# Three of four tile groups transposed by VectorE and transfers instead of TensorE, ahead of the third layer

## The chip, the cores and the metric

The kernel runs on one core of a Trainium2 chip. The metric is device time in microseconds. The kernel before took 707.68, 710.18 and 1081.44 us in three runs (median 710.18); the profiled execution took 706.28 us, of which the profile's span, from the first to the last instruction, is 704.5 us.

## The reference

The input u has 2048 positions of 512 channels. Two blocks follow each other, each ahead of a layer norm and added to its input:

```python
h  = u + ssm(layernorm(u))          # a long convolution by FFT, plus a skip term
h2 = h + mlp(layernorm(h))

def mlp(x):                         # w1, w2: 512x512, w3: 512x1792, w4: 1792x512
    g  = gelu(layernorm(x) @ w1)    # layer 1
    hs = shift(g) @ w2              # four quarters of the channels, shifted by +1 -1 +2 -2 positions; layer 2
    x1 = x + hs
    return x1 + gelu(layernorm(x1) @ w3) @ w4   # layers 3 and 4
```

Only the second block is touched here, and of it the way from x1 to layer 3, and the output.

## The kernel before, in words

The positions are held in 16 tiles of 128 positions by 512 channels (`h[:, j, :]`), in four groups q of four tiles. In a tile the 128 positions are not neighbours: position 16 p + j lies in row p of tile j up to a fixed order of the four row quarters (`ov`, line 1422), so that a shift by a position is a change of tile.

Numbers go into TensorE as a high and a low part (`split`, `gelu`, `halve`: ScalarE makes the high part, VectorE subtracts it for the low one), and a product is three matmuls (`PROD`, line 1170). Each part is a tile of 128 x 512 from the pool `slab`; temporaries come from the pool `tm` under the tags x (14 tiles) and g (6). TensorE writes into eight banks of PSUM: four that rotate (`bank`) and four that hold accumulators (`wide_bank`).

The first part of the program is the convolution, ordered by a planner (`Plan`). From about 310 us on comes `mixer_phase` (line 1127), whose order on TensorE, VectorE, ScalarE and GpSimd is that in which the Python code issues the instructions (`InOrder`): each engine works through its queue in that order. Transfers are issued by SyncE, some of the last output by ScalarE.

- Layer 1 (`layer1`, line 1219) and layer 2 (`layer2`, line 1257) are interleaved by hand in lines 1402 to 1420. `layer2(j)` writes x1 of tile j (`xq[j]`); `stats2` and `norm2` turn it into its layer norm, in place.
- Layer 3 needs the channels as rows, so each group is transposed by `turn2(q)` (line 1306): for each of four channel blocks c, four 128 x 128 transposes on TensorE against the identity into one bank, and one ScalarE copy into the tile `FT[q, c]` (128 channels by 512 positions).
- Layer 3 works on pairs of groups, as a 2 x 2 block product with seven products instead of eight (Strassen and Winograd): the operands are sums and differences of the blocks (`sums2`, line 1327) which `halve` splits, seven for each of two channel halves, so 28 slabs to a pair.
- The steps s = 0 to 13 (line 1520) run over seven pairs of column blocks of w3, for the first pair of groups (s = 0 to 6) and then for the second (7 to 13). A step does `layer3a(s)` (products a, b, c, e), layer 4 of the step before for its first half (`layer4a`), `layer3b(s)` (products f, d, g), and the second half (`layer4b`). Each product goes into a rotating bank, from which VectorE adds it (`plus`). Weights are loaded by `raw3` and `raw4` on SyncE, and split by `load3` and `load4`.

Group 0 is turned between layer1(2, 0) and layer1(2, 1) (line 1407), and its blocks b11 and b21 are halved after layer2(6) (lines 1408 to 1410). Group 1 is turned after layer2(10) (line 1411). Groups 2 and 3 belong to the second pair and are turned during the steps of the first: group 2 in step 2 (line 1541), group 3 half in step 3 and half in step 4 (line 1548); their sums are formed in steps 4 and 5, and halved around step 6 (`fresh`). In `todo` and `some` (line 1341) VectorE and ScalarE instructions are parcelled out between other work.

`store(j)` (line 1479) writes a finished tile to DRAM in four transfers of 32 rows each: on SyncE for the first pair, on SyncE and ScalarE in turn for the second.

Of the kernel before, what the change touches and what calls it, by code (L numbers as in the profile page):

```python
# [11 lines left out]
F32 = mybir.dt.float32  # L12
# [3 lines left out]
ALU = mybir.AluOpType  # L16
# [1110 lines left out]
def mixer_phase(ctx, tc, cst, h, out, finish, w3, w4):  # L1127

    nc = InOrder(tc)
    pool = lambda name, bufs, **kw: ctx.enter_context(tc.tile_pool(name=name, bufs=bufs, **kw))  # L1130
    sl = pool("slab", 45)
    tm = pool("tm", 6)
    w1p = pool("wrap", 1)
    sm = pool("sm", 2)
    ps = pool("ps2", 4, space=PSUM)
    pa = pool("pacc", 1, space=PSUM)
    ident = cst["ident"]
    NFT = F // 128

    def slab(name):  # L1140
        return sl.tile([128, 512], F32R, tag="slab", name=name)
# [1 line left out]
    def slot(i):  # L1143
        return cst["slab"](i)

    def tmp(name, tag):
        return tm.tile([128, 512], F32, tag=tag, name=name, bufs={"x": 14, "g": 6}[tag])

    def bank(name):
        return ps.tile([128, 512], F32, tag="bank", name=name)  # L1150

    def wide_bank(i, name):
        return pa.tile([128, 512], F32, tag=f"acc{i}", name=name)
# [7 lines left out]

    def gelu(b, name):

        hi, lo, g = slab(f"{name}h"), slab(f"{name}l"), tmp(f"g{name}", "g")
        nc.scalar.activation(hi, b, AF.Gelu_apprx_tanh)
        nc.scalar.activation(g, b, AF.Gelu_apprx_tanh)
        nc.vector.tensor_tensor(lo, g, hi.bitcast(F32), ALU.subtract)
        return hi, lo
# [6 lines left out]
    _, _, rr, nb = cst["norm"]  # L1175
# [30 lines left out]
    def norm1(q):  # L1206
        XL[q] = []
        for j in range(q * 4, q * 4 + 4):
            t = tmp(f"xl{j}", "x")
            if (q == 0 and j % 2) or (q == 3 and j != 14):  # L1210
                nc.vector.tensor_scalar(t, h[:, j, :], mv[:, j, 0:1], r12[:, j : j + 1], ALU.subtract, ALU.mult)
            else:
                nc.scalar.activation(t, h[:, j, :], AF.Identity, scale=r12[:, j : j + 1], bias=off12[:, j : j + 1])
            XL[q].append(t)
# [34 lines left out]
    def h1_block(f, j, k):  # L1249
        if 0 <= j < 16:  # L1250
            return H1[j // 4, f][k][:, j % 4 * 128 : j % 4 * 128 + 128]
        return wrap[k][WRAP[f, j] // 4][:, WRAP[f, j] % 4, :]

    xq = {}
    mv2 = {}

    def layer2(j):
        q, i = divmod(j, 4)
        b = bank(f"l2_{j}")
        n = 0  # L1260
        for f, sh in enumerate((-1, 1, -2, 2)):
            for wi, xi in PROD:
                nc.tensor.matmul(b, h1_block(f, j + sh, xi), W2[f][wi], start=(n == 0), stop=(n == 11))
                n += 1
        x1 = tmp(f"x1_{j}", "x")
        nc.vector.scalar_tensor_tensor(x1, h[:, j, :], r1[:, j : j + 1], b, ALU.mult, ALU.add)
        xq[j] = x1
        if j < 8:
            residual(j), stats2(j)

    def residual(j):
        (nc.gpsimd if j < 12 else nc.vector).tensor_tensor(h[:, j, :], h[:, j, :], xq[j], ALU.add)

    def stats2(j):
        q, i = divmod(j, 4)
        if q not in mv2:
            mv2[q] = sm.tile([128, 4, 2], F32, tag="mv2", name=f"mv2_{q}")
        st = sm.tile([128, 6], F32, tag="bst", name=f"st1_{j}")
        nc.vector.bn_stats(st, xq[j])
        nc.vector.bn_aggr(mv2[q][:, i, :], st)  # L1280
# [16 lines left out]
    def norm2(q):  # L1297
        for op in norm2_ops(q):
            op()
# [3 lines left out]
    half = NFT // 2  # L1303
    FT, XC, W3, W4 = {}, {}, {}, {}

    def turn2(q, cs=range(4), wide=True):

        tiles = [xq[q * 4 + i] for i in range(4)]
        for c in cs:
            b = wide_bank(c, f"x1t{q}_{c}") if wide else bank(f"x1t{q}_{c}")  # L1310
            for i, t in enumerate(tiles):
                nc.tensor.transpose(b[:, i * 128 : i * 128 + 128], t[:, c * 128 : c * 128 + 128], ident)
            FT[q, c] = tmp(f"ft{q}_{c}", "x")
            nc.scalar.copy(FT[q, c], b)

    def sub(out, a, b):
        nc.vector.tensor_tensor(out, a, b, ALU.subtract)
        return out

    def halve(src, pair, name, c, low=nc.vector):  # L1320

        hi, lo = slab(f"{name}{pair}{c}h"), slab(f"{name}{pair}{c}l")
        nc.scalar.copy(hi, src)
        low.tensor_tensor(lo, src, hi.bitcast(F32), ALU.subtract)
        XC[pair, name, c] = hi, lo

    def sums2(pair, c):

        S = FT[pair, "sums", c] = {}
        ft = lambda i, k: FT[pair * 2 + i, 2 * k + c]  # L1330
        t = lambda n: tmp(f"{n}_{pair}{c}", "xg"[pair == 0])

        def first():
            S.update(b11=ft(0, 0), b21=ft(0, 1), b22=ft(1, 1), t1=sub(t("t1"), ft(1, 0), ft(0, 0)))

        return [first, lambda: S.update(t3=sub(ft(1, 0), ft(1, 1), ft(1, 0))),
                lambda: S.update(t2=sub(t("t2"), S["b22"], S["t1"])), lambda: S.update(t4=sub(t("t4") if pair else S["b21"], S["b21"], S["t2"]))]
# [70 lines left out]
    for n in ("b11", "b21"):  # L1408
        for c in range(2):
            halve(FT[0, c + 2 * (n == "b21")], 0, n, c)  # L1410
    layer2(7), norm2(1), layer2(8), layer2(9), layer2(10), turn2(1)
    rest = []
    for c in range(2):
        t1, t3, t2, t4 = sums2(0, c)
# [7 lines left out]
    ov = out.rearrange("(a c j) d -> c a j d", c=4, j=16)  # L1422
    acc, H3, U = {}, {}, {}

    def prod(s, name, w, xk):
        b = bank(f"l3{name}_{s}")
        for n, (c, wi, xi) in enumerate((c, wi, xi) for c in range(2) for wi, xi in PROD):
            nc.tensor.matmul(b, W3[s][w][wi][:, c * 128 : c * 128 + 128], XC[s // half, xk, c][xi], start=(n == 0), stop=(n == 5))
        return b
# [10 lines left out]
        return lambda: nc.vector.tensor_tensor(lo, src, hi.bitcast(F32), ALU.subtract)  # L1440

    def layer3a(s):
        U[s] = [tmp(f"u{i}_{s}", "g") for i in range(4)]
        one, two, three, last = U[s]
        nc.scalar.copy(one, prod(s, "a", "a11", "b11"))
        if s == 0:

            f, e, c = (prod(s, n, *o) for n, o in (("f", ("a12", "b21")), ("e", ("s1", "t1")), ("c", ("s3", "t3"))))
            plus(last, f, one)
            for i in (0, 2, 1, 3):  # L1450
                rest[i]()
            load3(1, nc.vector, range(1))
            plus(two, prod(s, "b", "s2", "t2"), one)
            plus(three, c, two)
            plus(one, e, three)
            plus(two, e, two)
            U[s] = last, two, three, one
            return
        plus(two, prod(s, "b", "s2", "t2"), one)
        plus(three, prod(s, "c", "s3", "t3"), two)  # L1460
        b = prod(s, "e", "s1", "t1")
        plus(last, b, three)
        plus(two, b, two)
# [13 lines left out]
        return gelu3(s, 0, 1, two)  # L1477

    def store(j):
        for c in range(4):  # L1480
            queue = nc.scalar if j >= 8 and c % 2 else nc.sync
            queue.dma_start(ov[c][:, j, :], h[c * 32 : c * 32 + 32, j, :])

    def layer4(s, q, i, b, first, last):
        for k in range(2):
# [34 lines left out]
    for s in range(2 * half):  # L1520
        turn, last = s + 1 == half, s + 1 == 2 * half
        layer3a(s)
        if turn:
            fresh(("b11", "t2", "t3", "t1"))
        if last:
            load4(s)
        else:
            load3(s + 1, *((nc.gpsimd,) if s else (nc.vector, range(1, 3))))
        if s + 2 < 2 * half:
            raw3(s + 2)  # L1530
        if s:
            layer4a(s - 1)
        if s == 0:
            for j in range(8, 12):
                residual(j)
        if s == 1:
            for j in range(8, 12):
                stats2(j)
            todo.extend(norm2_ops(2)), some(11)
        if s == 2:  # L1540
            turn2(2, range(4), False)
            for j in range(12, 16):
                if j > 13:
                    residual(j)
                stats2(j)
            todo.extend(norm2_ops(3)), some(11)
        if s == 3 or s == 4:
            turn2(3, (s - 3, s - 1), False)
        if s == 4 or s == 5:
            todo.extend(sums2(1, s - 4))  # L1550
            some(4)
        late = layer3b(s)
        if not last and s:
            load4(s), raw4(s + 1)
        if s + 2 < 2 * half:
            sum3()
        if s:
            layer4b(s - 1, late)
        else:
            late()  # L1560
        some(4)
        if s == 1:
            residual(12), residual(13)
        if turn:
            fresh(("b21", "t4", "b22"))
# [45 lines left out]
```

## Time and profile before

| | before |
|---|---|
| runs | 707.68, 710.18, 1081.44 us |
| profiled execution | 706.28 us |
| its span | 704.5 us |
| TensorE busy | 667.0 us (95%) |
| VectorE busy | 539.7 us (77%) |
| ScalarE busy | 413.1 us (59%) |
| GpSimd busy | 393.9 us (56%) |
| granted TensorE clock, mean | 0.992 |

How to read the profile's lines: PE is TensorE's matmuls, PEld its weight loads, DVE VectorE, ACT ScalarE, POOL GpSimd, SP SyncE; SPq is SyncE's queue, which issues transfers. All times are microseconds from the start of the span, or nanoseconds where it says ns. An instruction is named by the tile that it writes and those that it reads, as in `x1t<-ident,x`. Where the kernel's helper records an instruction, all of them bear one line number (L87), so groups are told apart by their tiles: `x1t` are the banks of `turn2`, `ft` its result, `l3a` to `l3g` the seven products of layer 3, `l` the rotating banks of layers 1, 2 and 4, `acc` the accumulators of layer 4, `u` the temporaries of layer 3. In square brackets stands how long the engine was idle before an instruction, and what ended it. The chain that ended last is followed back from the last instruction, at each step to what released it. A matmul's shown duration overlaps with the next one's.

### The profile page before, as it was taken

What the parts mean: (1) busy time and instruction counts of PE and PEld (TensorE: products, weight loads), DVE (VectorE), ACT (ScalarE), POOL (GpSimd) and SP (SyncE); (2) the same over time, 40 slices, a digit from 0 to 9 for tenths busy, and PEclk for the clock granted to TensorE, in tenths of its full rate; (3) what the DMA queues carried; (4) which work ended last, traced back from release to release, by engine and by line L of the source; (5) the groups of instructions that cost most, each with busy time, mean ns of one, the idle gap of its engine ahead of it and who ended that gap; (6) DMA issues with size and microseconds to landing.
All of it is one profiled execution on the core that took longest, in us unless ns stands there. A gap on an engine that the chain in (4) does not pass through costs nothing.

```text
span 704.5 us, 16738 instructions
## 1 busy us (share of the span) xinstructions
PE 667.0 (95%) x6894; PEld 522.0 (74%) x6894; DVE 539.7 (77%) x934; ACT 413.1 (59%) x701; POOL 393.9 (56%) x407
## 2 busy tenths in 40 slices
PE   5878999999999989989999999999999999999997
PEld 5865666663776774848888888888888888888886
DVE  6998899999999898878764889846568954554544
ACT  7888778765889875245646346554545544444330
POOL 1889587967999897302555404555433655543310
PEclk9999999999999999999999999999999999999999
DMA  8830653010301133010010001221111352111004
GB/s 215 268 121 3 197 166 78 3 47 32 63 2 47 33 92 107 1 61 1 1 30 31 1 16 45 61 60 54 39 59 31 87 154 60 51 52 48 10 21 120
DMA packets 44912, 45.19 MB, mean 64 GB/s; under 512 B 4900, under 2 KB 31524, under 8 KB 44836
## 3 DMA queue, kind: packets, MB, share of 16 engines
q1 hardware_dynamic: 44068, 43.07, 21.0%
q10 hardware_dynamic: 768, 1.05, 0.6%
q8 instruction: 54, 0.88, 0.5%
q14 instruction: 22, 0.18, 0.1%
HBM read 35.72 MB, written 8.39 MB: 63 GB/s over the span
## 4 chain that ended last, share of the span: by engine, by line
PE 63%; DVE 17%; ACT 9%; DMA 4%; issue 3%; POOL 2%; SPq 1%; DVEq 0%; ACTq 0%; POOLq 0%
PE l L87 23%; PE acc L87 11%; PE bank L87 9%; ACT pt L87 5%; DVE at L87 3%; DVE u L87 3%; DVE cs L87 3%; PE l3c L87 3%; PE l3f L87 3%; PE l3e L87 3%; PE l3d L87 3%; PE l3b L87 3%; PE l3g L87 3%; PE l3a L87 3%; DVE sn L87 2%
## 5 line engine op out<-in xcount | busy, mean ns | idle before, releaser
L87 ACT ACTIVATE pt<-pt 128x1056 f32<-128x1056 int32 x64 | 69.9, 1092 | 17.2 <-POOL pt L87 7.8
L87 POOL TENSOR_TENSOR pt<-p,s 128x512 int32<-128x512 int32 x64 | 71.5, 1133 | 5.6 <-DVE sn L87 5.3
L87 PE MATMUL bank<-at,tbs 128*64 128x128 f32 (+1 forms) x768 | 64.5, 317 | 2.0 <-DVE at L87 1.0
L87 PEld LDWEIGHTS bank<-at,tbs 128*64 128x64 f32 x768 | 46.3, 138 | 18.8 <-ACT at L87 2.3
L87 PEld LDWEIGHTS bank<-ident 128*128 128x128 f32 x438 | 54.4, 204 | 7.2 <-issue 4.4
L87 PE MATMUL bank<-ident 128*128 128x128 f32 x438 | 58.4, 292 | 0.0
L87 PE MATMUL bank<-u,ms 64*128 64x128 f32 x736 | 49.4, 281 | 4.8 <-POOL u L87 2.0
L87 PEld LDWEIGHTS bank<-u,ms 64*128 64x128 f32 x736 | 43.7, 187 | 9.8 <-POOL u L87 3.1
L87 POOL TENSOR_TENSOR cs0w<-raw,cs0w 128x512 fp32r<-128x512 f32 x7 | 9.1, 1299 | 64.4 <-ACT cs0w L87 64.4
L87 DVE TENSOR_TENSOR h<-h,l 128x512 f32<-128x512 f32 x48 | 32.6, 687 | 14.7 <-PE l L87 14.7
L87 DVE TENSOR_TENSOR u<-u,l3f 128x512 f32<-128x512 f32 x14 | 9.6, 686 | 44.5 <-PE l3f L87 44.5
L87 POOL TENSOR_TENSOR cs1w<-raw,cs1w 128x512 fp32r<-128x512 f32 x7 | 9.1, 1299 | 61.0 <-ACT cs1w L87 61.0
L87 DVE TENSOR_TENSOR cs<-pt,amx 128x512 f32<-128x512 f32 x64 | 41.2, 680 | 2.4 <-ACT pt L87 1.8
L87 PE MATMUL bank<-cs 128*32 128x64 f32 x1024 | 32.7, 224 | 8.1 <-DVE cs L87 6.3
L87 PEld LDWEIGHTS bank<-cs 128*32 128x32 f32 x1024 | 24.2, 111 | 20.7 <-ACT kt L87 4.3
L87 ACT COPY at<-bank 128x512 f32<-128x512 f32 x40 | 24.7, 624 | 24.8 <-PE bank L87 24.8
L87 ACT ACTIVATE pt<-pt,halfpi 128x1056 f32<-128x1056 f32 x32 | 37.8, 1182 | 0.7
L87 DVE STREAM_TRANSPOSE at<-bank 128x512 f32<-128x512 f32 (+1 forms) x40 | 35.0, 909 | 3.5 <-PE bank L87 3.5
L87 ACT ACTIVATE u<-u 128x512 f32<-128x512 f32 x56 | 35.4, 633 | 1.8
L87 DVE TENSOR_TENSOR amx<-E,amx 128x896 f32<-128x896 f32 (+1 forms) x32 | 30.7, 959 | 5.6 <-ACT amx L87 5.4
L87 POOL TENSOR_TENSOR sn<-pt,amp 128x512 f32<-128x512 f32 x27 | 32.7, 1210 | 2.8 <-ACT pt L87 1.4
L87 PE MATMUL bank<-sn 128*32 128x64 f32 x1024 | 31.9, 223 | 2.2 <-DVE sn L87 1.6
(1161 smaller groups left out, 2096.1 us busy)
## 6 DMA issues: line engine op xcount, KB each, us to landing
raw<-in_B_w_dram SPq DMA_DIRECT2D x28, 256.0 KB, 2.6
h<-in_A_u_dram SPq DMA_DIRECT2D x32, 128.0 KB, 4.2
h<-in_A_u_dram SPq DMA_DIRECT2D x16, 256.0 KB, 4.2
rawa<-in_B_w_dram SPq DMA_DIRECT2D x14, 256.0 KB, 2.7
rawb<-in_B_w_dram SPq DMA_DIRECT2D x14, 256.0 KB, 2.7
ms<-in_mm_dram SPq DMA_DIRECT2D x4, 768.0 KB, 10.7
out_dram<-h SPq DMA_DIRECT2D x48, 64.0 KB, 1.7
xs<-far SPq DMA_DIRECT2D x10, 256.0 KB, 2.9
```

The lines of the kernel that those rows point to most:

```text
L87: ins = f(*args, **kw)
```

## The change

For groups 0, 2 and 3 `turn2` no longer uses TensorE, PSUM and ScalarE. VectorE transposes each tile in blocks of 32 x 32 within its four row quarters (four instructions of 128 x 512), and the blocks change rows by way of a DRAM buffer `via[q]`: four transfers write it (each run 512 bytes), four read it back (each run 2 KB) over the tiles of x1. All eight are issued by SyncE. The numbers come back in an order in which a channel block c lies in runs of 32 numbers, `turned` names it, and `natural` restores the order of positions where the sums and halves are formed. `FT[q, c]` is now such a view and no tile of its own.

Group 1 keeps TensorE (`turn2_wide`), and ScalarE copies its result over the tiles of x1, in the same order. Group 3 is turned wholly in step 3.

The tiles under the tag x become four fixed tiles of 128 x 2048, `XQ`, used in turn by the norms of layer 1, by x1, by the block transposes and by the sums of the second pair. The pool g goes from 6 to 5 tiles, and slab from 45 to 44. `store` writes a tile in two transfers of 64 rows.

```diff
-    sl = pool("slab", 45)
+    sl = pool("slab", 44)
...
+    dp = pool("via", 1, space=bass.MemoryType.DRAM)
+    via = {q: dp.tile([128, 2048], F32, name=f"via{q}") for q in (0, 2, 3)}
...
-    def tmp(name, tag):
-        return tm.tile([128, 512], F32, tag=tag, name=name, bufs={"x": 14, "g": 6}[tag])
+    def tmp(name):
+        return tm.tile([128, 512], F32, tag="g", name=name, bufs=5)
+
+    XQ = [w1p.tile([128, 4 * 512], F32, name=f"xq{i}") for i in range(4)]
+    X1 = {0: XQ[3], 1: XQ[1], 2: XQ[2], 3: XQ[0]}
+    quarter = lambda t, i: t[:, i * 512 : i * 512 + 512]
+    turned = lambda t, q: t.rearrange("p (a c i t) -> p c a i t" if q == 1 else "p (a i c t) -> p c a i t", a=4, c=4, i=4)
+    natural = lambda t: t.rearrange("p (i a t) -> p a i t", i=4, a=4)
...
-            t = tmp(f"xl{j}", "x")
+            t = quarter(XQ[{3: 0, 0: 1, 1: 2, 2: 0}[q]], j % 4)
...
-        x1 = tmp(f"x1_{j}", "x")
+        x1 = quarter(X1[q], i)
...
-    def turn2(q, cs=range(4), wide=True):
+    def turn2(q):
+
+        x, t = X1[q], XQ[{0: 2, 2: 3, 3: 1}[q]]
+        for i in range(4):
+            nc.vector.transpose(quarter(t, i).rearrange("p (b c t) -> p c b t", b=4, c=4),
+                                quarter(x, i).rearrange("p (c b t) -> p c b t", c=4, b=4))
+            nc.sync.dma_start(via[q].rearrange("p (b i x) -> p b i x", b=4, i=4)[:, :, i, :],
+                              quarter(t, i).rearrange("p (b x) -> p b x", b=4))
+        for a in range(4):
+            nc.sync.dma_start(quarter(x, a), via[q].rearrange("(a d) (b x) -> a b d x", a=4, b=4)[a])
+        for c in range(4):
+            FT[q, c] = turned(x, q)[:, c]
+
+    def turn2_wide(q):
 
         tiles = [xq[q * 4 + i] for i in range(4)]
-        for c in cs:
-            b = wide_bank(c, f"x1t{q}_{c}") if wide else bank(f"x1t{q}_{c}")
+        for c in range(4):
+            b = wide_bank(c, f"x1t{q}_{c}")
             for i, t in enumerate(tiles):
                 nc.tensor.transpose(b[:, i * 128 : i * 128 + 128], t[:, c * 128 : c * 128 + 128], ident)
-            FT[q, c] = tmp(f"ft{q}_{c}", "x")
-            nc.scalar.copy(FT[q, c], b)
+            FT[q, c] = turned(X1[q], q)[:, c]
+            nc.scalar.copy(FT[q, c], natural(b))
...
-        nc.scalar.copy(hi, src)
-        low.tensor_tensor(lo, src, hi.bitcast(F32), ALU.subtract)
+        nc.scalar.copy(natural(hi), src)
+        low.tensor_tensor(natural(lo), src, natural(hi).bitcast(F32), ALU.subtract)
...
-        t = lambda n: tmp(f"{n}_{pair}{c}", "xg"[pair == 0])
+        home = lambda n: quarter(XQ[(3, 1)[c]], "t1 t2 t4".split().index(n)) if pair else tmp(f"{n}_{pair}{c}")
+        t = lambda n: home(n).rearrange("p (a i t) -> p a i t", a=4, i=4)
...
-    layer2(7), norm2(1), layer2(8), layer2(9), layer2(10), turn2(1)
+    layer2(7), norm2(1), layer2(8), layer2(9), layer2(10), turn2_wide(1)
...
     def store(j):
-        for c in range(4):
-            queue = nc.scalar if j >= 8 and c % 2 else nc.sync
-            queue.dma_start(ov[c][:, j, :], h[c * 32 : c * 32 + 32, j, :])
+        for c in (0, 2):
+            queue = nc.scalar if j >= 8 and c else nc.sync
+            queue.dma_start(ov[c : c + 2, :, j, :], h[c * 32 : c * 32 + 64, j, :])
...
         if s == 2:
-            turn2(2, range(4), False)
+            turn2(2)
...
-        if s == 3 or s == 4:
-            turn2(3, (s - 3, s - 1), False)
+        if s == 3:
+            turn2(3)
```

More of the change, by code (lines that the diff above doesn't have):

```diff
@@ L1162, in gelu @@
     def gelu(b, name):
-        hi, lo, g = slab(f"{name}h"), slab(f"{name}l"), tmp(f"g{name}", "g")
+        hi, lo, g = slab(f"{name}h"), slab(f"{name}l"), tmp(f"g{name}")
         nc.scalar.activation(hi, b, AF.Gelu_apprx_tanh)
@@ L1442, in layer3a @@
     def layer3a(s):
-        U[s] = [tmp(f"u{i}_{s}", "g") for i in range(4)]
+        U[s] = [tmp(f"u{i}_{s}") for i in range(4)]
         one, two, three, last = U[s]
```

## The prediction

> **What bounds the kernel now.** The page comes first: span, busy shares and the chain of work that ended last.
>
> ```profile
> span 704.5 us, 16738 instructions
> PE 667.0 (95%) x6894; PEld 522.0 (74%) x6894; DVE 539.7 (77%) x934; ACT 413.1 (59%) x701; POOL 393.9 (56%) x407
> PE 63%; DVE 17%; ACT 9%; DMA 4%; issue 3%; POOL 2%; SPq 1%; DVEq 0%; ACTq 0%; POOLq 0%
> ```
>
> The busy share is an average, so the second view is the same chain in order of time, around the four second transposes (x1t). Columns: start, duration, what.
>
> ```profile
> 371.46 1.75 PE x1t L87 x16
> 373.21 21.86 PE l L87 x96
> 395.07 1.78 PE x1t L87 x16
> ...
> 422.79 1.67 PE l3c L87 x6
> ...
> 451.70 1.75 PE x1t L87 x16
> 453.45 1.37 PE l3f L87 x6
> ...
> 473.87 0.87 PE x1t L87 x8
> ...
> 495.19 0.87 PE x1t L87 x8
> ```
>
> Each piece starts where the one before ends: TensorE sets the end here. Group 0 is the piece at 371.46, group 1 (which stays) 395.07, group 2 451.70, group 3 the two halves. The waits of TensorE's weight loads from 360 to 530 us say how near another engine is:
>
> ```profile
> PEld l3c L87 <- DVE u L87: 0.5, 1, 0.5
> PEld l L87 <- DVE h_3l L87: 0.2, 1, 0.2
> ```
>
> Two waits only, both for VectorE. So no slack shows, and VectorE is the next bound, at 422 us above all.
>
> **What leaves TensorE.** 48 transposes: 1.75 us in group 0, 1.75 in group 2, 0.87 twice in group 3, together 5.24 us. The tile view gives their single durations:
>
> ```profile
> L87 PE MATMUL x1t<-ident,x x64: 270/272/308, 371.3 to 495.8; 128*128 128x128 f32 x64
> L87 ACT COPY ft<-x1t x16: 586/592/640, 372.5 to 496.1; 128x512 f32<-128x512 f32 x16
> ```
>
> They overlap: sixteen take 1.75 us on the chain, 109 ns each, and only that can be saved. ScalarE loses 12 copies of 0.59 us, which are on no chain piece above: nothing.
>
> [...]
>
> **What comes in, group 0.** VectorE's queue before the change, with the copies of ScalarE that follow:
>
> ```profile
> 372.69 0.69 DVE L87 TENSOR_TENSOR h_0l<-gh,h_0h 128x512 fp32r<-128x512 f32 x1 [1.32 <-ACT gh L87]
> 377.19 0.69 DVE L87 TENSOR_TENSOR h_1l<-gh,h_1h 128x512 fp32r<-128x512 f32 x1 [3.81 <-ACT gh L87]
> ...
> 385.81 1.05 DVE L87 TENSOR_TENSOR b1100l<-ft,b1100h 128x512 fp32r<-128x512 f32 x1
> ...
> 387.39 0.68 DVE L87 TENSOR_TENSOR b2100l<-ft,b2100h 128x512 fp32r<-128x512 f32 x1
> 388.00 0.68 DVE L87 TENSOR_TENSOR b2101l<-ft,b2101h 128x512 fp32r<-128x512 f32 x1
> 388.60 0.74 DVE L87 SCALAR_TENSOR_TENSOR x<-h,rr,l 128x512 f32<-128x512 f32 x1
> ```
>
> ```profile
> 382.43 0.62 ACT L87 CAST b1100h<-ft 128x512 fp32r<-128x512 f32 x1
> 392.82 2.23 ACT L87 ACTIVATE x<-x,qo,qr 128x512 f32<-128x512 f32 x3 [8.22 <-DVE qo L87]
> ```
>
> The four block transposes queue behind h_0l, into the 3.81 us of idle time. The same instruction in the convolution, and the rows that bound the transfers (groups by form, queues and a window):
>
> ```profile
> L87 DVE STREAM_TRANSPOSE at<-bank 128x512 f32<-128x512 f32 x24 | 15.5, 687 | 0.7 <-PE bank L87 0.7
> L87 DVE TENSOR_TENSOR h<-h,bank 128x512 f32<-128x512 f32 x4 | 2.7, 682 | 0.0
> far<-xs SPq DMA_DIRECT2D x4, 256.0 KB, 2.1
> h<-in_A_u_dram SPq DMA_DIRECT2D x4, 256.0 KB, 4.8
> raw<-in_B_w_dram SPq DMA_DIRECT2D x2, 256.0 KB, 2.6
> 312.00:316.00 4.00, 3.92 (x25) 3.22 (x26) 4.00 (x10) 2.67 (x5) 0.00 (x0) 1.00 0.80 251
> 363.90 0.38 SPq L1354 DMA_DIRECT2D rawb<-in_B_w_dram  x1
> 379.06 1.59 SPq L1383 DMA_DIRECT2D raw<-in_B_w_dram  x2
> ```
>
> Instructions of 0.68 us follow each other every 0.61 us (387.39, 388.00), so the transposes run from 373.3 to 375.8. SyncE's queue is free by then (last issue 363.90). Four writes are issued at 374.1 to 375.9, 0.38 us each. One write of 256 KB lands in 2.1 us, four issued together in 4.8 (the median of four), and 251 GB/s, the last column of the window, is 4.2 us per MB. I take 374.1 + 2.1 + three quarters of 4.2 = 379.4 for the last of the four (bounds 378.0 and 380.7: the last issue and 2.1 or 4.8). The reads wait for all four: issued from 379.5, last landing 379.5 + 2.6 + 3.1 = 385.2, which I call **T**. Bounds by the same rows: 381.7 (last issue 379.3, and 2.4) and 387.2.
>
> Behind T wait ScalarE's copies of the four halves (b11, b21) and, in VectorE's order, four subtractions, then layer2(7)'s x, its statistics and the root that tile group 1 needs for its norm. The copy and the subtractions take 0.62 + 0.1 + 3 x 0.61 + 0.68 = 3.3 us with the hand-over. From the end of the last subtraction (388.68) to group 1's transposes (395.07) went 6.4 us. So TensorE can start these at T + 9.7 = 394.9, where it would now be there at 395.07 - 1.75 = 393.3. It waits 1.6 us: of the 1.75 us, **0.2 us** stays (bounds: 1.75 where T is 383.6 or less, -1.8 at 387.2). layer2(7) to (10) have four banks and run on meanwhile. The two weight loads on SyncE (379.06) are pushed behind the reads to about 381; they feed layer 3's step 1 at 420 us: nothing. The stretch from there to 422.79 hangs on VectorE and moves with group 1, as a whole.
>
> **Group 2, step 2.** VectorE's queue and TensorE's wait there:
>
> ```profile
> 449.10 1.04 DVE L87 TENSOR_TENSOR h<-h,x 128x512 f32<-128x512 f32 x1
> ...
> 454.39 0.17 DVE L87 SCALAR_TENSOR_TENSOR qo<-mv,qr 128x4 f32<-128x4 f32 x1
> 454.85 0.69 DVE L87 TENSOR_TENSOR u<-u,l3f 128x512 f32<-128x512 f32 x1 [0.30 <-PE l3f L87]
> ...
> 476.16 0.69 DVE L87 TENSOR_TENSOR u<-u,l3f 128x512 f32<-128x512 f32 x1 [6.42 <-PE l3f L87]
> ```
>
> Here the transposes stand ahead of the statistics, additions and root that end at 454.6: four at 0.61 put them 2.45 us later, and the sum that empties l3f's bank begins at 457.0 rather than 454.85. TensorE, 1.75 us early, does l3f, l3d, l3g and the first layer-4 tile (1.36 us each) in four banks from 451.70, and at 457.1 wants l3f's bank again, which comes free at 457.8: it waits 0.7 us, and **1.05 us** stays. Bounds: 1.75 with no wait; at 1.04 us each, the duration of a VectorE addition at 449.10 beside a busy GpSimd, it waits 2.3 us and loses 0.5. The transfers have until step 4: nothing.
>
> **Group 3.** In step 3 VectorE idles 6.42 us ahead of l3f: four transposes fit, and 0.87 + 0.87 = **1.74 us** stays. SyncE's writes stand behind the weight loads there; the result is wanted at 490.98:
>
> ```profile
> 469.97 0.38 SPq L1354 DMA_DIRECT2D rawb<-in_B_w_dram  x1
> 490.98 0.85 DVE L87 TENSOR_TENSOR t<-ft,ft 128x512 f32<-128x512 f32 x1
> ```
>
> Writes begin at 470.4, and T - 374.1 = 11.1 us later is 481.5, so some 9 us of cover are left, minus the 1.7 us by which TensorE is ahead.
>
> **Reordered tiles.** Additions and copies on them go in runs of 32 numbers. h<-h,bank above has just such runs (32 columns of each of 16 tiles) and takes 682 ns, as the contiguous subtractions at 387.39 and 388.00: nothing.
>
> **Stores.** At the end each queue issues one transfer where it issued two:
>
> ```profile
> L1482 SPq DMA_DIRECT2D out_dram<-h x48: 314/422/494, 559.5 to 701.3; - x48
> DMA to landing us min/median/max: 1.6/1.8/2.7
> ```
>
> One issue of 0.42 us goes, and 128 KB lands between 1.8 (64 KB) and 2.6 us (256 KB); I take 2.0, so **0.2 us** (bounds 0.4 and -0.4).
>
> **Pools.** One slab and one g tile fewer: layer 3's sets in use, 28 halves and 16 for two steps, are the 44 that are left. Nothing, with up to 1 us of loss if a tile is awaited.
>
> **Sum.** 0.2 + 1.05 + 1.74 + 0.2 = 3.2 us off 706.28 (span 704.5 and 1.78 around it): 703.1. That execution is the lowest of those shown; the next stands 1.40 above, the median (710.18) 3.90. A timed run should stand higher too, so I forecast 703.1 + 1.4 = **704.5**. What a measurement of this kernel can tell from no change I put at 2%.
>
> **Rivals.** (B) All is covered: T is at most 383.6 and step 2 makes no wait: 5.24 + 0.2 off, 700.8 + 1.4 = 702.2. For: single transfers land in 2.1 to 2.6. Against: four at once took 4.8.
> (C) The gain is given back, 707.7: VectorE, late by what it is given, holds TensorE in group 0 and step 2 (bounds above), or the copies of group 1, which now write into the tiles that its transposes still read, are ordered one after the other: 0.44 + 0.59 + 0.1 per part, four times, is 2.4 us more on TensorE than the 1.78 + 0.3 now.
> (D) Slower: the round trip of group 0. Each microsecond of T beyond 388.4 (385.2 + 3.2) is a loss. Writes and reads of about 7 us each, half as long again as the longest median, make T 390.5: TensorE waits until 400.2, the loss is 5.3 - 3.2 = 2.1, so 709.8. For: everything hangs on two serial transfers with no other cover. Against: no row so long. Beyond 2% it takes a T of 402.
> [...]
>
> [...]
>
> (E) The transposes cost TensorE their single durations: 13.1 saved, 693.2 + 1.4 = 694.6. The chain excludes it nearly.
>
> **How the numbers follow.** Forecast (702.8 to 706.5) 0.45, B 0.15, C 0.18, D 0.20, E 0.02. The range takes in B from 701, C, and D without its far tail: 701 to 711. Faster by over 2% is E with 0.01 beside it for a mistake of mine; slower by over 2% is D's far tail, 0.05; the rest, 0.93, is within.
>
> **What would show it.** The chain has x1t once, at about 395, with TensorE waiting for ScalarE's norm ahead of it some 1.6 us; the reads of group 0 land near 385; l3f's bank is awaited once in step 2; 473.87 and 495.19 close without a wait. Wrong if T is far off, or if a wait shows on the reordered tiles.

## The result, and the profile after

The changed kernel takes 755.44 us (median of 6 runs, 755.26 to 760.55) against 709.15 us for the kernel before (median of 6). The ratio of the means is 1.0678, with a 95% interval from 1.0635 to 1.0721. It is slower, and 44 us above the upper end of my range. The ratios here leave out the one run of 1081.44 us; the other executions of every kernel, the one before too, fall into two clusters some 5 us apart, a difference that arises ahead of the mixer (its start lies between 309.7 and 315.2 us in the profiled executions) and whose cause stays open.

The page of the changed kernel's profile answers to the first fence of the prediction:

```profile
span 758.8 us, 16652 instructions
PE 669.9 (88%) x6846; PEld 521.8 (69%) x6846; DVE 546.0 (72%) x946; ACT 406.6 (54%) x689; POOL 393.7 (52%) x407
PE 52%; DVE 19%; ACT 9%; DMA 5%; issue 4%; POOL 3%; SPq 2%; ACTq 0%; DVEq 0%; POOLq 0%
```

48 matmuls are gone, yet TensorE is busy for 2.9 us more, in a span that is 54.3 us longer. TensorE's share of the chain fell from 63 to 52%. It waits now, and some of its matmuls are stretched.

To find the places, I set the same milestones of both chains side by side: the first product of a layer 3 step (l3a), and the last addition. The chain before, in order of time (start, duration, what):

```profile
410.50 1.36 PE l3a L87 x6
440.81 1.36 PE l3a L87 x6
462.98 1.36 PE l3a L87 x6
...
505.60 1.36 PE l3a L87 x6
...
566.89 1.36 PE l3a L87 x6
...
607.69 1.36 PE l3a L87 x6
...
700.21 0.69 DVE h L87
```

The same chain after, with the pieces that lead to the late ones:

```profile
383.35 10.88 DMA xq<-via
...
403.91 3.25 PE x1t L87 x14
407.16 14.88 PE l L87 x60
422.04 1.36 PE l3a L87 x6
...
452.31 1.36 PE l3a L87 x6
...
473.11 1.36 PE l3a L87 x6
...
513.91 1.36 PE l3a L87 x6
...
575.20 1.36 PE l3a L87 x6
...
606.18 9.64 DMA rawb<-in_B_w_dram
...
623.58 5.12 PE l L87 x12
628.70 1.39 PE l3a L87 x6
...
721.26 0.69 DVE h L87
```

The mixer's start is the first transpose of layer 1, before and after:

```profile
311.93 1.94 PE L87 MATMUL xt<-ident,xl 128*128 128x128 f32 x16 [1.32 <-ACT h L87]
314.20 1.94 PE L87 MATMUL xt<-ident,xq 128*128 128x128 f32 x16 [1.33 <-ACT h L87]
```

Subtracting the milestones gives the whole difference of these two executions (706.28 and 760.55 us):

| stretch | before | after | difference |
|---|---|---|---|
| start to the mixer (no part of the change) | 311.93 | 314.20 | +2.3 |
| to step 0 of layer 3 (group 0 turned) | 98.57 | 107.84 | **+9.3** |
| steps 0 and 1 | 30.31 | 30.27 | 0 |
| step 2 (group 2 turned) | 22.17 | 20.80 | **-1.4** |
| steps 3 and 4 (group 3 turned) | 42.62 | 40.80 | **-1.8** |
| steps 5 to 7 | 61.29 | 61.29 | 0 |
| steps 8 and 9 (stores of the first pair) | 40.80 | 53.50 | **+12.7** |
| step 10 to the last addition | 92.52 | 92.56 | 0 |
| end of the last addition to the end of the span | 3.6 | 36.9 | **+33.2** |

Groups 2 and 3 do what was forecast. Group 0 costs 9.3 us, and the stores, which I had put at a gain of 0.2 us, cost 45.9 us in two places. TensorE's waits from 360 us on name two of these places (engine, tile and what it waited for; total, times, longest, in us); before had none there for the matmuls:

```profile
PE l L87 <- DVE u L87: 10.3, 1, 10.3
PE x1t L87 <- ACT xq L87: 7.2, 3, 6.7
```

VectorE and ScalarE are only the last hand here: behind both, the chain shows a transfer. SyncE's queue in order of time says what the transfers stood behind:

```profile
379.78 1.59 SPq L1405 DMA_DIRECT2D raw<-in_B_w_dram  x2
381.55 2.32 SPq L1323 DMA_DIRECT2D xq<-via  x4
...
567.27 0.38 SPq L1376 DMA_DIRECT2D rawb<-in_B_w_dram  x1
567.75 17.18 SPq L1504 DMA_DIRECT2D out_dram<-h  x10
...
601.72 4.36 SPq L1376 DMA_DIRECT2D rawa<-in_B_w_dram  x1
...
712.51 25.76 SPq L1504 DMA_DIRECT2D out_dram<-h  x8
```

A weight load is issued in 0.38 us at 567.27. Behind the first pair's stores an issue takes 4.36 us (601.72): here SyncE itself is held up. `rawa` and `rawb` are here the layer 3 weights of step 10, which `raw3` issues in step 8, behind the stores. ScalarE works in order and has their splitting ahead of step 9's results, so it stands still first:

```profile
615.04 0.62 ACT L87 CAST ptw<-rawa 128x512 fp32r<-128x512 f32 x1 [15.00 <-DMA rawa<-in_B_w_dram]
```

VectorE, which takes its next operand from these results, is idle for 12.9 us, and TensorE waits for the bank that VectorE's following sum empties (u at 622.85). The last pair's stores are issued from 712.5 on, eight here and eight by ScalarE.

The windows say why the queue is held up. Columns: window, busy us of PE, PEld, DVE, ACT, POOL with counts, granted clock, DMA share, GB/s.

```profile
379.00:382.00 3.00, 3.00 (x15) 2.49 (x14) 1.24 (x1) 1.18 (x3) 3.00 (x3) 1.00 0.97 266
383.40:394.20 10.80, 10.79 (x48) 8.63 (x47) 2.32 (x4) 0.00 (x0) 2.50 (x3) 1.00 0.25 98
400.00:404.00 4.00, 1.03 (x3) 0.45 (x4) 3.65 (x12) 2.22 (x3) 1.07 (x1) 0.50 0.00 0
575.00:584.00 9.00, 9.00 (x41) 7.44 (x41) 4.45 (x8) 3.94 (x7) 8.92 (x9) 1.00 0.14 52
730.00:758.00 28.00, 0.00 (x0) 0.00 (x0) 0.00 (x0) 0.00 (x0) 0.00 (x0) 0.50 0.13 49
```

Read the column before the last. While the reads of `via` are all that moves, the DMA share, a mean over the 16 engines, is 0.25: as much as 4 of them. While SyncE issues the first pair's stores (575 to 584) it is 0.14, and at the end, where nothing but stores runs, 0.13: as much as 2 of 16, there although two queues issue them. The writes of `via` (379 to 382, with a weight load behind them) reach 0.97. The shapes of the three transfers have these numbers in them. A store of the changed kernel goes to `ov[c : c + 2, :, j, :]`, 2 x 32 rows, so its outermost dimension is 2. A read comes from `via[q]` as "b d x", 4 x 32 rows: outermost 4. A write is 128 rows. Before, a store was 32 rows, and at the end of its span (of these three microseconds the last is empty, and 701 to 703 has 0.78 and 196 GB/s):

```profile
701.00:704.00 3.00, 0.00 (x0) 0.00 (x0) 0.00 (x0) 0.00 (x0) 0.00 (x0) 0.94 0.52 131
```

My theory for the experiments (**N**): a transfer is served by at most as many DMA engines as the outermost dimension of its DRAM side counts. It is drawn from the two shares above, 0.13 with 2 and 0.25 with 4; the share is a mean, so that just 2 or 4 engines work is the theory's reading of it. Sixteen stores of 128 KB are 2.1 MB; at 49 GB/s they take 43 us, and 712.5 + 43 = 755.5 is close to the end of the span (758.8). The reads, 1 MB at 98 GB/s, take 10.7 us: the 10.88 of the chain.

The rival explanations: (S) the stores are innocent and the lost time comes from the round trips (VectorE, SyncE and DRAM busy with `via`); (L) the reads are slow from their latency or from being few and large.

### The profile page after: what moved, and what is told of

Its sections match the earlier page's. It is cut to its first block, busy times and chain, and to the rows that moved or that the text cites. A ratio compares the mean times of both kernels' runs of the same rounds, so it can differ in the third digit from the quotient of the medians.

```text
span 758.8 us, 16652 instructions
## 1 busy us (share of the span) xinstructions
PE 669.9 (88%) x6846; PEld 521.8 (69%) x6846; DVE 546.0 (72%) x946; ACT 406.6 (54%) x689; POOL 393.7 (52%) x407
## 3 DMA queue, kind: packets, MB, share of 16 engines
q10 hardware_dynamic: 528, 1.05, 0.4%
## 4 chain that ended last, share of the span: by engine, by line
PE 52%; DVE 19%; ACT 9%; DMA 5%; issue 4%; POOL 3%; SPq 2%; ACTq 0%; DVEq 0%; POOLq 0%
PE l L87 19%; PE bank L87 9%; PE acc L87 9%; ACT pt L87 5%; DVE u L87 4%; DVE at L87 3%; DVE cs L87 3%; DMA h<-in_A_u_dram 2%; DVE sn L87 2%; PE l3c L87 2%; PE l3e L87 2%; PE l3a L87 2%; PE l3b L87 2%; PE l3f L87 2%; DVE amx L87 2%
## 5 line engine op out<-in xcount | busy, mean ns | idle before, releaser
L87 PEld LDWEIGHTS bank<-cs 128*32 128x32 f32 x1024 | 24.2, 111 | 20.2 <-ACT kt L87 4.3
L87 POOL TENSOR_TENSOR cs<-pt,amp 128x512 f32<-128x512 f32 x26 | 32.6, 1253 | 2.0 <-PE bank L87 0.7
```

The lines of the kernel that those rows point to most:

```text
L87: ins = f(*args, **kw)
```

## The experiments

None of these kernels leaves out any part of the computation. Where less than 1% matters I read the stretch of the chain beside the median. Levels differ between sessions: the kernel before has 709.15, 704.79 and 708.01 us. The expectations count from 705 to 709 us, so they are compared by ratio or by the chain.

### e1_stores4: the change with the old stores

```diff
 # against the changed kernel
-        for c in (0, 2):
-            queue = nc.scalar if j >= 8 and c else nc.sync
-            queue.dma_start(ov[c : c + 2, :, j, :], h[c * 32 : c * 32 + 64, j, :])
+        for c in range(4):
+            queue = nc.scalar if j >= 8 and c % 2 else nc.sync
+            queue.dma_start(ov[c][:, j, :], h[c * 32 : c * 32 + 32, j, :])
```

> The changed kernel with the output stored in four transfers per tile again. Theory N (narrow transfers: a transfer whose DRAM side begins with a dimension of n entries is served by n of the 16 DMA engines; two for a store of 2 x 32 rows, four for a read of 4 x 32 rows): in the changed kernel the stores cost 12.7 us in the middle and 33.2 us at the end, so this takes 755.4 - 45.9 = 709.5 us, and the span ends some 4 us after the last VectorE addition. Rival S (the stores only wait behind other traffic, which the round trips cause): it stays near 755.

Measured 709.22 us (10 runs) against 704.79 for the kernel before in that session (22 runs): ratio 1.0039 (1.0009 to 1.0070). The stores alone were 755.44 - 709.22 = 46.2 us across the two sessions, and some 45 us by the two ratios, as the 45.9 of the table. That the 709.5 expected was met so closely is in part luck, since the kernel before stood 4.4 us lower here; the chain counts: 393.42 us from the mixer's start to the last addition, against 388.28 before, 5.1 us lost. TensorE's wait for group 0 is unchanged, with the same reads on the chain (10.93 us, landing at 395.14).

### e2_stores2: the kernel before with the new stores

```diff
 # against the kernel before: the same edit, the other way round
+        for c in (0, 2):
+            queue = nc.scalar if j >= 8 and c else nc.sync
+            queue.dma_start(ov[c : c + 2, :, j, :], h[c * 32 : c * 32 + 64, j, :])
```

> The kernel before with nothing changed but the stores, two transfers of 64 rows. Theory N: 709.2 + 45.9 = 755 us, DMA share 0.13 (2 of 16) after the last VectorE addition. Rival S: without the round trips the stores are harmless, 709 us.

Measured 748.9 us (4 runs), ratio 1.0617 (1.0554 to 1.0679): without any round trip, the stores alone cost 44 us (45.9 expected), and S falls. This kernel's window after its last addition, and TensorE's only wait from 360 us on:

```profile
715.00:745.00 30.00, 0.00 (x0) 0.00 (x0) 0.00 (x0) 0.00 (x0) 0.00 (x0) 0.51 0.13 51
```

```profile
PE l L87 <- DVE u L87: 10.2, 1, 10.2
```

Both marks of the changed kernel are there: a share of 0.13 at the end, and a wait of 10.2 us in the middle.

### e4_store1: one store per tile, 4 x 32 rows

If engines follow the outermost dimension, half as many transfers with twice the dimension must be twice as fast; if fewer and larger transfers were the fault, this would be worse still.

```diff
 # against the kernel before
-        for c in range(4):
-            queue = nc.scalar if j >= 8 and c % 2 else nc.sync
-            queue.dma_start(ov[c][:, j, :], h[c * 32 : c * 32 + 32, j, :])
+        queue = nc.scalar if j >= 8 and j % 2 else nc.sync
+        queue.dma_start(ov[:, :, j, :], h[:, j, :])
```

> The kernel before with one store of 128 rows per tile (DRAM side 4 x 32 rows), every other one of the second half on ScalarE. Theory N: four of 16 engines, 0.25 DMA share and some 102 GB/s, twice the rate of the two-transfer store: the last eight tiles, 2.1 MB, take 20.5 us from the first of them, which ends some 11 us later than before the change, and the middle loses 0 to 3: 716 to 719 us against 705 before. Rival B (the cost goes with the size of a transfer: 64 KB in before, 128 KB in the changed kernel, 256 KB here): not below the 749 of e2.

Measured 716.31 us (one run). The window at its end:

```profile
700.00:710.00 10.00, 0.00 (x0) 0.00 (x0) 0.00 (x0) 0.00 (x0) 0.00 (x0) 0.60 0.26 102
```

A share of 0.26, as much as four engines, 102 GB/s, and the stretch behind the last addition is 15.9 us (698.57 to 714.5), between the 3.6 of four stores and the 36.4 of e2 (710.97 to 747.4). In the middle nothing is lost (steps 8 and 9 take 40.80 us, as before). Fewer and larger transfers are not the fault.

### e8_reads2: each read split into two of 2 x 32 rows

The same question for the reads, on top of e1: N says two engines and half the rate, L says no worse.

```diff
 # against e1
         for a in range(4):
-            nc.sync.dma_start(quarter(x, a), via[q].rearrange("(a d) (b x) -> a b d x", a=4, b=4)[a])
+            for b in (0, 2):
+                nc.sync.dma_start(quarter(x, a)[b * 32 : b * 32 + 64],
+                                  via[q].rearrange("(a d) (b x) -> a b d x", a=4, b=4)[a, b : b + 2])
```

> As e1, but each read of the round trips is split into two of 2 x 32 rows, eight of 128 KB. Theory N: two engines serve each, and the same two, as in the stores; 1 MB takes 20.5 us instead of 10.9, group 1's transposes start some 9.6 us later, 719 us. Rival L (latency of a read after a write, or too few reads in flight): more and smaller reads in flight land sooner or as late, 709 us or less.

Measured 744.67 us (one run). The window of the reads, and the waits:

```profile
385.00:405.00 20.00, 11.70 (x51) 9.31 (x50) 1.65 (x4) 0.00 (x0) 1.91 (x2) 0.86 0.13 51
```

```profile
PE x1t L87 <- ACT xq L87: 17.7, 3, 17.2
PE l L87 <- DVE u L87: 16.3, 1, 16.3
```

The reads of group 0 landed at 405.6 us instead of the 395.1 of e1, and TensorE's wait grew from 6.7 to 17.2 us: N holds, L falls. The size I had expected was still wrong, by the second wait. On the chain it hangs on this piece:

```profile
519.60 13.90 DMA xq<-via
```

These are the reads of group 3, for which the prediction saw some 9 us of cover. In the changed kernel that cover is already used up: VectorE waits ahead of the group's first sum, though TensorE does not:

```profile
503.70 0.69 DVE L87 TENSOR_TENSOR xq<-xq,xq 128x512 f32<-128x512 f32 x1 [3.43 <-DMA raw<-in_B_w_dram]
```

The load named there is only the transfer that ended last by the profile; with the wide reads of e3 and e5 VectorE has no wait at this place. In e8 the same sum begins 29.25 us after the start of step 4, in e1 9.06. Of these 20.2 us, 9.2 are the first read's later issue, since the issues ahead of it on SyncE are slower (the four writes 6.66 us, 2.63 in e1), and 11.0 the longer time from there to the sum (24.6 us against 13.6). I had counted group 0 alone.

### e3_rows: round trips in wide transfers

The same blocks, written by four transfers of 32 rows and read by four of 128 rows, so that no outermost dimension on the DRAM side is below 32. The writes come behind all four block transposes.

```diff
 # against e1
-            nc.vector.transpose(quarter(t, i).rearrange("p (b c t) -> p c b t", b=4, c=4),
+            nc.vector.transpose(t.rearrange("p (b i c t) -> p i c b t", b=4, i=4, c=4)[:, i],
                                 quarter(x, i).rearrange("p (c b t) -> p c b t", c=4, b=4))
-            nc.sync.dma_start(via[q].rearrange("p (b i x) -> p b i x", b=4, i=4)[:, :, i, :],
-                              quarter(t, i).rearrange("p (b x) -> p b x", b=4))
+        blocks = via[q].rearrange("(a r) (s x) -> a (r s) x", a=4, s=4)
+        for a in range(4):
+            nc.sync.dma_start(blocks[a].rearrange("(b d) x -> d b x", b=4), t[a * 32 : a * 32 + 32].rearrange("p (b x) -> p b x", b=4))
         for a in range(4):
-            nc.sync.dma_start(quarter(x, a), via[q].rearrange("(a d) (b x) -> a b d x", a=4, b=4)[a])
+            nc.sync.dma_start(quarter(x, a), blocks[a])
```

> As e1, and the round trips with another order in DRAM: four writes of 32 rows x 4 runs of 2 KB after all four block transposes, four reads of 128 rows of 2 KB. Theory N: reads and writes run on 16 engines, the reads of group 0 land some 7 to 9 us earlier, TensorE's wait ahead of group 1 falls from 6.7 us to 0 to 3, its clock stays at 1.00, and the time is 704 to 708 us. Rival L (the round trip is long because a read of DRAM follows a write to it, whatever the shape): 709.5 us as e1, with the wait of 6.7 us unchanged.

Measured 702.45 us (10 runs), ratio 0.9956 (0.9918 to 0.9993). The chain, and a window of the writes and of the reads:

```profile
379.67 4.75 DMA via<-xq
...
384.49 2.87 DMA xq<-via
...
412.34 1.36 PE l3a L87 x6
```

```profile
380.00:381.00 1.00, 1.00 (x6) 0.81 (x5) 0.56 (x1) 0.41 (x1) 1.00 (x1) 1.00 1.00 211
384.50:387.30 2.80, 2.80 (x13) 2.26 (x13) 1.62 (x3) 0.00 (x0) 1.62 (x2) 1.00 0.99 346
```

Behind the last write, reads of the same megabyte take 2.87 us rather than 10.9, at a share of 0.99, and the writes of 32 rows fill the engines too (1.00). A read has the same bytes, runs of 2 KB and 128 rows of SBUF as in e1; of its shape, only the DRAM side's outermost dimension differs, 128 against 4. (In DRAM its rows now lie together, too, where they lay 8 KB apart; but per busy engine such reads were no slower: 98 GB/s at 0.25 in the changed kernel, 346 at 0.99 here.) They land at 387.36; the mixer of this execution starts 2.43 us later than in the profile before (314.36), so T is 384.9 in the prediction's frame, where I had 385.2. TensorE's wait is down from 6.7 us to 0.4. From the mixer's start to step 0 of layer 3 it takes 97.98 us, 0.6 less than before. So the missing term in group 0 was the shape of the transfers, all of it. e3 also changes the writes and puts the two weight loads behind the reads (384.86); that the reads are the term is shown by their time here and by e8.

### e6_g0pe: group 0 back on TensorE

```diff
 # against e1
-    turned = lambda t, q: t.rearrange("p (a c i t) -> p c a i t" if q == 1 else ...
+    turned = lambda t, q: t.rearrange("p (a c i t) -> p c a i t" if q < 2 else ...
...
-    layer1(2, 0), turn2(0), layer1(2, 1), ...
+    layer1(2, 0), turn2_wide(0), layer1(2, 1), ...
```

> As e1, and group 0 transposed by TensorE again, groups 2 and 3 still by VectorE and the slow reads. If the cost of the round trips is the late arrival of group 0 alone, 709.2 - 1.4 (group 2) - 1.7 (group 3) = 706 us, and no wait of TensorE over 1.5 us from 360 to 560 us. If narrow reads also hold up the weight loads behind them, 709 us or more.

Measured 700.94 us (7 runs), ratio 0.9936 (0.9885 to 0.9986); the 706 us expected are a ratio of 0.9955 in their session. By the chain from the mixer's start to the last addition it gains 3.3 us (384.96 us). Its chain in group 1 shows the transposes and the copies into tiles that the transposes still read, at their old pace:

```profile
396.70 1.78 PE x1t L87 x16
398.48 13.64 PE l L87 x60
```

Beside the changed kernel this gives the price of the clock. There 14 of the 16 transposes take 3.25 us and the following 60 matmuls 14.88; here 16 take 1.78 and the 60 take 13.64. That is about 1.5 + 1.2 = 2.7 us, the two transposes done during the wait counted in its favour, behind an idle time of

```profile
402.50 0.47 PE L87 MATMUL x1t<-ident,xq 128*128 128x128 f32 x1 [6.72 <-ACT xq L87]
```

6.72 us, with a granted clock of 0.50 in the changed kernel's window from 400 to 404 (0.50 from 404 to 408 too, 0.79 from 408 to 412, 1.00 from 412 to 416; in e6 1.00 from 385 to 396). It is the price of this execution: in e1, behind an equal wait, the same two pieces take 3.25 and 14.02 us, 1.9 us more than here (e1's clock there is not shown), and in e8, behind 17.2 us and at 0.50 from 405 to 420, the transposes take 3.25 and 47 of the 60 (up to 430) 11.44, where e6's pace gives 10.68: 2.2 us more.

### e5_g0pe_rows and e7_late2: what can be had

e5 joins e6 and the wide round trips of e3 for groups 2 and 3 (the edits are those two). e7 adds to it that group 2's block transposes are issued at the end of step 2, behind the statistics:

```diff
 # e7 against e5
         if s == 2:
-            turn2(2)
             for j in range(12, 16):
...
         some(4)
+        if s == 2:
+            turn2(2)
```

> As e6 (group 0 by TensorE, four stores), with the wide round trips of e3 for groups 2 and 3. If the narrow reads of groups 2 and 3 are wholly covered, the same as e6: 3.1 us less than before (1.4 in step 2, 1.7 in steps 3 and 4), ratio 0.9955. If they cost something, 1 us or more below e6.

> As e5, with group 2's block transposes at the end of step 2 instead of ahead of its statistics. If the statistics, put 2.5 us later, are what keeps 0.36 of group 2's 1.75 us, step 2 is 20.4 us long instead of 20.8 in the chain, and the time is 0.4 us below e5, which the timing cannot tell; if the transposes only move the wait to step 3, step 3 is longer by as much.

Measured 701.09 us for e5 (12 runs), ratio 0.9927 (0.9896 to 0.9957), and 700.56 us for e7 (12 runs), ratio 0.9936 (0.9901 to 0.9971); the kernel before had 708.01 there (23 runs). e5 equals e6: where groups 2 and 3 alone go by DRAM, e6's narrow reads cost TensorE nothing: it has no wait from 360 us on in either. The change of e7 is visible in its chain alone, in step 2 (439.89 to 460.30) and the step behind it:

```profile
439.89 1.36 PE l3a L87 x6
460.30 1.36 PE l3a L87 x6
480.69 1.36 PE l3a L87 x6
```

Step 2 takes 20.41 us instead of 20.80, and step 3, which now has the transposes' end beside it, is no longer for that (20.39): the 0.4 us of wait that the block transposes caused there are gone. In the medians this can't be seen. e5, e6 and e7 beat the kernel before by 0.6 to 0.7%, and can't be told apart; the simplest is e6, two lines of code and the old stores.

## Why the prediction was wrong

**The stores: the step that failed.** "One issue of 0.42 us goes, and 128 KB lands between 1.8 (64 KB) and 2.6 us (256 KB); I take 2.0, so 0.2 us". The rows were true, but they belong to stores of 32 rows and loads of 128. I interpolated over bytes, and here the shape set the rate (49 GB/s at the end, 196 before). Measured: a loss of 45.9 us (e2 alone: 44.1). I also looked for the cost at the end only; 12.7 us of it lie in steps 8 and 9, where SyncE's queue carries the first pair's stores ahead of the weight loads: 10.3 us of wait, and 12 matmuls in 5.12 us (granted clock 0.50 from 624 to 628) that take 2.72 at a granted clock of 1.00 (24 in 5.44 at 634.18), 2.4 us. Of a tile with two stores, the prediction should have asked what is behind them on SyncE, as it did for the round trips.

**Group 0: T.** "One write of 256 KB lands in 2.1 us ... last landing 379.5 + 2.6 + 3.1 = 385.2". Measured 394.23 in the changed kernel, 392.0 in the prediction's frame (its mixer starts 2.27 us later). The writes were right: they ran at 0.97 of the engines, and the reads' issue began at 381.55, or 379.3 in that frame. The reads were the error, 12.7 us from the first issue to the last landing instead of 5.7, again by shape. e3 with wide reads has T at 384.9.

The rest of the step held. From T to group 1's transposes I had 9.7 us; the chain shows 394.23 to 403.91. With T at 392.0, the prediction's own chain gives a loss of 392.0 - 385.2 - 0.2 = 6.6 us, and the clock 2.7 (e6): 9.3, which is what the table shows. In e1 the same pieces took 1.9 us longer than in e6, and the same stretch grew by 8.4. Rival D thus had the mechanism ("Each microsecond of T beyond 388.4 (385.2 + 3.2) is a loss"), with a price that was too low: it has no term for the clock, and I let a transfer be half as slow again and not twice.

**Where the clock halved.** In the kernel before, 1.32 us of idle time ahead of 311.93 left the granted clock at 1.00 (the window from 312 to 316). In the changed kernel it was 0.50 behind the idle time of 6.72 us, and the pieces behind it took 2.7 us longer than in e6.

**Group 2.** Predicted 1.05 us kept; measured 1.37. TensorE's wait was 0.4 us and not 0.7: step 2 took 20.80 us, against 20.41 in e7 without it. The place was right. Here TensorE's second tile of layer 4 waits for the VectorE sum that empties l3f's bank; in the chain and in VectorE's queue after:

```profile
468.69 4.42 PE l L87 x18
```

```profile
467.95 0.68 DVE L87 TENSOR_TENSOR u<-u,l3f 128x512 f32<-128x512 f32 x1
```

18 of the 24 matmuls are left at 468.69, so the first tile is done and the second begins there, just behind the sum's end.

**Group 3.** Predicted 1.74, measured 1.82; but the cover I had seen was not there: the writes began 10.4 us into step 3 (483.51) and not 7.4, the reads were slower, and VectorE's first sum waited 3.43 us (the row in e8). TensorE was not reached by it.

**Block transposes.** Predicted 2.45 us for four, right behind h_0l; measured 2.48, from 375.55 on.

**Reordered tiles.** Nothing predicted, and nothing found: VectorE's subtractions on runs of 32 numbers take 0.68 us after as before (b1101l at 395.64), and e6 shows group 1's copies without a wait, which drops that half of rival C.

**Weight loads.** I had raw4's two loads pushed behind the reads. They went ahead of them (loads from 379.78, reads from 381.55 in SyncE's queue), and the second, by the chain, waited for GpSimd until 381.0 and held the reads up behind it. The reads couldn't have begun much sooner, since the writes and the first weight load kept the engines busy until about then (0.97 from 379 to 382); how much of it was the wait, no run tells apart.

**The sum.** Even without the stores it would have missed: e1 loses 5.1 us by the chain where a gain of 3.0 was forecast. Without the stores and with wide reads, the prediction's forecast of 704.5, from an execution of 706.28 plus 1.4, is a gain of 3.2 us, 3.0 of it without the stores; e3 measured a ratio of 0.9956, 3.1 us (0.5 to 5.8 by its interval), and by the chain 3.8 us (384.44 us from the mixer's start to the last addition, against 388.28). The method of the sum stood; two terms were priced from transfers of another shape. A slip without effect: its chances for faster by over 2%, slower by over 2% and within (0.03, 0.05 and 0.93) add up to 1.01.

**What stays open:** how many transfers a queue takes before its engine is held up; and a store in two transfers with a wide outermost dimension, which was not tried.

## What to carry to other kernels

When a transfer is rewritten, write down its access pattern's outermost dimension on the DRAM side before its bytes: here, with stores of 2 x 32 rows for stores of 32, the DMA share at the end fell from 0.78 (701 to 703 before) to 0.13. In a profile, look for a DMA share that stands flat while something waits for a transfer: here 0.13 and 0.25 were this fault. Then look at what the queue behind the slow transfer carries: here the weight loads behind the first pair's stores were late too, and steps 8 and 9, far from the place of the edit, took 12.7 us more.

## What the runs showed of the hardware

- Per busy engine the narrow stores and reads moved some 25 GB/s: 49 to 51 GB/s at a share of 0.13 (the changed kernel, e2, e8), 98 to 102 at 0.25 and 0.26 (the changed kernel, e4). The wide reads moved 22 (346 at 0.99, e3), the stores of 32 rows 16 (196 at 0.78, before, 701 to 703), the writes of `via` 17 (266 at 0.97, the changed kernel, with a weight load behind them) and 13 (211 at 1.00, e3).
- The narrow stores of two queues didn't add up: SyncE's and ScalarE's at the end of the changed kernel and of e2 together used 0.13, and those of e4 0.26.
- SyncE was held up by its queue's slow stores: an issue took 0.38 us at 567.27 and 1.7 us on the mean over the next ten stores, and a weight load 4.36 us behind them.
- Behind an idle time of TensorE of 6.7 us the pieces of group 1 took 2.7 us longer than in e6 (the changed kernel, granted clock 0.50 from 400 to 408) and 1.9 us (e1, clock not shown), and behind one of 17.2 us 2.2 us (e8, 0.50 from 405 to 420). Behind the wait of 10.3 us in step 9, 12 matmuls took 2.4 us longer (0.50 from 624 to 628).
